# A fused attention and two mixture-of-experts layers: shares laid out by expert, two conversions and a scaling in another order, one earlier load

## The chip, the cores and the metric

The kernel runs on one core of a Trainium2 chip. A core has five engines that work side by side: TensorE (PE in the profile; PEld is its loading of weights), VectorE (DVE), ScalarE (ACT), GpSimd (POOL) and SyncE (SP, which here only issues transfers). Each engine takes its instructions in program order and waits where a semaphore is not there yet. The metric is the device time in microseconds of one execution. Three runs of the kernel before gave 1183.86, 1184.28 and 1185.43 us; their median is 1184.28.

## The reference

Attention over 2 batches of 8 heads with 576 positions and a bias that a small network computes from the positions; on its output (1152 tokens of 512 values) a dense layer with 2048 hidden values and softplus; on that, eight experts with 1024 hidden values each, whose outputs are added with shares P that eight rounds of normalisation make from a gate:

```python
logits = x @ w_gate                      # 1152 x 8
P = np.exp(logits - logits.max())
for _ in range(8):
    P /= P.sum(1, keepdims=True) + 1e-09
    P /= P.sum(0, keepdims=True) + 1e-09
    P *= N / E
for e in range(E):
    out += P[:, e:e + 1] * (np.maximum(x @ w1[e], 0.0) @ w2[e])
```

## The kernel before

*Stages.* The program is written out by hand: each engine's order is the order in which the code issues its instructions, and nothing is rearranged. The first 100 us make the attention's bias: 40 row groups n = 0 to 39 (in `bias_emit`), each summed on TensorE, stored to the DRAM scratch `wt` (five row tiles; wt_72 to wt_76 in the orders below) and read back as `bias` for the first pair of heads at the row groups that the table `READS` names. Other work is hung into these groups by a dictionary `late`: what stands under n is issued after group n's sums and before the reads of that group. Then come eight pairs of heads, nine soft steps s each, which a generator issues (`attention`); its first step, s = 0, is itself issued from `late` at n = 39. `load(i, "kr")` brings the keys of pair i with two transfers of 288 KB on SP's queue into a buffer `raw`; `prep` turns them into a high part `ks` (VectorE, L366) and low parts (POOL, L417).

*Experts.* A unit u is 256 hidden columns: units 0 to 7 are the dense layer, units 8 to 39 the experts, four units each. Every product is computed in three terms from a high part (the operand rounded to fp32r) and a low part (what rounding left): high x high, high x low, low x high. A high part is a copy by ScalarE (`first`, L857), a low part a subtraction by POOL or VectorE (`second`, L861). From unit 12 on, where the experts' shares are ready, units are *gated*: the hidden values are multiplied with the share of their token (VectorE, L880), and units 12 to 38 run the second matrix product in seven half-size products instead of eight (`down_fast`, list `DOWN`), from the hidden blocks B11, B12, B21, B22 and their differences T1 to T4. TensorE runs such a unit in some 22.4 us: the seven products of the up projection (`product`, L818), then the seven of `DOWN` (L994), in the order at = 0 to 6; the product at = 0 needs B11, at = 4 T3, at = 5 B21, at = 6 T4. A unit's start is meant below as the transposition in `turn_last`, behind at = 0.

*Weights.* SP loads a unit's weights into `f` two units ahead. `parts` splits them: ScalarE copies a half to the high part (L730) and, negated, to the low part (L734), and a transfer on POOL's queue then adds the weights to the low part (L735). `weights["high"](u, 1)` is this for the second half of the up weights `wu`, `"highd"` for the down weights `wd`, `"highs"` for the down weights' differences, whose low part lies in `room`. In a unit, POOL issues three of these transfers one behind the other: `wu` of the unit after the next, `wd` and `room`.

*Shares.* `publish` stores the shares from SBUF into the DRAM scratch `pt`, a row of 128 tokens for each pair of token tile t and expert e, row t * 8 + e. `share_of(e, c)` reads half c of expert e's shares back into all 128 partitions (`pb`, 512 tokens); `shares_of` reads both halves. `publish` reads expert 1's two halves and, between them, expert 0's two halves into `raws[2]` and a part of `fs[2]`. `shares_of` is issued at the last unit of an expert, six times, ahead of the next expert. The products of expert 0 (units 8 to 11) went into the accumulators without shares; `weigh_columns` multiplies these accumulators with expert 0's shares in unit 12 (the first scaling, L1038): two on VectorE, two on POOL.

Of the kernel before, what the change touches and what calls it, by code (L numbers as in the profile page):

```python
# [25 lines left out]
E = 8  # L26
# [27 lines left out]
FIRST_STEPS = (39,)  # L54
TABLE_AT = 33
FIRST_LOAD = 3
READS = ((30, 2, ((0, 576),)), (31, 1, ((0, 512),)), (34, 0, ((0, 384),)), (36, 1, ((512, 576),)), (39, 0, ((384, 576),)),
         (39, 3, ((0, 576),)), (39, 4, ((0, 576),)))
G_BUFS = 2
# [54 lines left out]
def attention_moe_moe_kernel(ctx: ExitStack, tc, qT, kT, vN, wpos, w_in, w_out, w_gate, e_w1, e_w2,  # L114
                             psi, logd, rpsi, place, out):
    nc = tc.nc
# [318 lines left out]
    def attention(env, pre, biases, read, ep, bp):  # L435
        pairs, state, load, prep, fixed = pre
# [134 lines left out]
        for s in range(len(seq) + LAG + 2):  # L571
            if s <= AHEAD_STEPS:
                yield
            if s == AHEAD_STEPS:
                sp, xr, beside = env
                for w in range(2):
                    ts = [sp.tile([128, 4, 128], F32R, tag=f"v{x}{w}", name="vx") for x in "hl"]
                    for x in ts:
                        nc.gpsimd.memset(x[:, :, 64:128].bitcast(F32), 0.0)
                    fixed.append(ts)  # L580
            i, r = divmod(s, NT)
            r_now[0] = r
            for w in ORDER[r]:
                if w == "t" and 0 <= s - LAG < len(seq):
                    transp(*seq[s - LAG])
                elif w == "q" and s + 1 < len(seq):
                    qk(*seq[s + 1])
                elif w == "p":
                    for n in range(at[s - 1] if s else 0, at[s]):
                        pv(*parts[n])  # L590
            if LOWFIRST[r]:
                for f in lows:
                    f()
                lows.clear()
            if s < len(seq):
                soft(*seq[s])
            for f in tails + lows:
                f()
            tails.clear()
            lows.clear()  # L600
            if 0 <= s - 1 < len(seq):
                norm(*seq[s - 1], (r - 1) % NT)
            if s == 0:
                load(1, "kr")
            if s == 2:
                prep(0, 5, sp)
            for k, at_r in enumerate(PREPS if i else PREPS1):
                if at_r == r:
                    prep(i + 1, k, sp)
            if r == VLOAD and i + 1 < len(pairs):  # L610
                load(i + 1, "v", sp)
            if i // 2 + 1 < HP and (i % 2, r) in AHEAD:
                read(i // 2 + 1, AHEAD[i % 2, r])
            if s >= AHEAD_STEPS:
                beside(s, ep)


    def experts(m0, accp, xr):
# [6 lines left out]
        U1 = F1 // 256  # L625
# [358 lines left out]
        def down_fast(u):  # L984
# [3 lines left out]
            for at, (n, x, a, b, (c, i)) in enumerate(DOWN):  # L988
# [11 lines left out]
                    nc.vector.tensor_tensor(out=d, in0=banks[x][:, fs_], in1=d, op=ALU.add)  # L1000
                if at == 0:
                    turn_last(u)
                    if u > U1 + UE:
                        weights["high"](u + 1, 1)
                    later.pop()()
                    if (u + 1 - U1) % UE == 0:
                        shares_of((u + 1 - U1) // UE)
                    difference(nc.gpsimd, "T4", "B21", "T2")
                    first("T3")
                    second(nc.gpsimd, "T3")  # L1010
                    second(nc.gpsimd, "B21")
                if at == (2 if u == U1 + UE else 0):
                    if len(tss) < 3:
# [232 lines left out]
        def publish():  # L1246
# [1 line left out]
            tt, sb = bank("t"), raws[2][:, 512:640]  # L1248
            nc.tensor.transpose(tt[0:NT * E, 0:128], pool["prob"].rearrange("p t e -> p (t e)"), ident)
            nc.vector.tensor_copy(sb[0:NT * E], tt[0:NT * E, 0:128])  # L1250
            nc.sync.dma_start(out=pool["pt"], in_=sb[0:NT * E])
            pb["first", 0], pb["first", 1] = raws[2][:, 0:512], fs[2][:, 512:1024]
            for c in range(2):
                share_of(1, c)
                nc.sync.dma_start(out=pb["first", 1 - c].rearrange("p (t n) -> p t n", n=128), in_=shares(0, 4 * (1 - c), 4))

        def shares(e, t, n):
            src = pool["pt"][:]
            return bass.AP(tensor=src.tensor, offset=src.offset + (t * E + e) * 128, ap=[[0, 128], [128 * E, n], [1, 128]])

        def share_of(e, c):
            pb[c] = pool["moe"].tile([128, 512], F32, tag=("s3", "lgt")[c], bufs=1, name="pb")
            nc.sync.dma_start(out=pb[c].rearrange("p (t n) -> p t n", n=128), in_=shares(e, 4 * c, 4))

        def shares_of(e):
            for c in range(2):
# [97 lines left out]
        def unit(u):  # L1364
# [64 lines left out]
            else:  # L1429
                for n, p in enumerate(UP_FAST if fast(u) else UP):  # L1430
                    if u == U1 + UE and n == 5:
                        tss.extend(again(k, [128, 2, 512], F32R) for k in range(2))
                        for i in range(2):
                            weigh_columns(nc.gpsimd, 0, 1 - i)
                    if n == 3 and u == U1 + UE:
                        weigh_columns(nc.vector, 1, 0)
                    if n == 6 and u == U1 + UE:
                        weights["high"](u + 1, 1)
                    if n > 1:
# [115 lines left out]
    with tc.manual_schedule(), ExitStack() as stack:  # L1555
# [37 lines left out]
        one = cst.tile([128, 1], F32, name="one")  # L1593
        late.setdefault(TABLE_AT, []).append(lambda: nc.scalar.activation(one, ident[:, 0:1], AF.Exp))
        late.setdefault(FIRST_LOAD, []).append(lambda: load(1, "qr"))
        for n in FIRST_STEPS:
            late.setdefault(n, []).append(lambda: next(steps))
        with tc.tile_pool(name="btmp", bufs=1) as sp, tc.tile_pool(name="bg", bufs=1) as gp, tc.tile_pool(
# [73 lines left out]
```

## Time and profile before

| what | value |
|---|---|
| median of 3 runs | 1184.28 us (1183.86 to 1185.43) |
| profiled execution | 1183.7 us |
| its span, first to last instruction | 1181.9 us |
| granted clock of TensorE | 1.000 |
| TensorE busy (PE) | 1146.2 us, 97% of the span |
| weight loads (PEld) | 958.6 us, 81% |
| VectorE | 878.2 us, 74% |
| POOL | 840.9 us, 71% |
| ScalarE | 724.6 us, 61% |

The page of the profile describes one execution, whose span is 1.8 us shorter than the execution's own time. TensorE is the fullest engine; it is busy in nearly every slice of the span but the first two. The other engines' idle time costs only where TensorE waits for it. A row of a timeline gives the start in us, the duration, the engine, the line of the code, the operation and its operands; in brackets stands how long the engine was idle before it and what ended that. Rows that follow each other directly are merged, with their count behind an x. TensorE's end times are modelled, and a matmul starts before the one ahead of it has ended, so pairs of rows overlap.

### The profile page before, as it was taken

The page shows a single profiled execution, that of the slowest core. Times are in us where ns is not written, and L with a number is a line of the kernel's source. Part 1 is how long each engine was busy: PE and PEld are TensorE (multiplying, and loading weights), DVE is VectorE, ACT ScalarE, POOL GpSimd, SP SyncE. Part 2 cuts the span into 40 slices and gives each one's busy share as a digit, 9 for nine tenths or more (in the row PEclk, how much of TensorE's full clock was granted, in tenths as well). Part 3 has the DMA queues.
Part 4 walks back from the last instruction along what each step waited for, and adds up shares of the span by engine and source line. Part 5 has one row for each costly group of instructions (what it writes and reads, how often), then busy time and mean ns, then how long its engine had stood idle before and what let it go on. Part 6 is the DMA issues. An engine that isn't in the chain of part 4 may idle for free.

```text
span 1181.9 us, 19793 instructions
## 1 busy us (share of the span) xinstructions
PE 1146.2 (97%) x7289; PEld 958.6 (81%) x7289; DVE 878.2 (74%) x1469; ACT 724.6 (61%) x1190; POOL 840.9 (71%) x858
## 2 busy tenths in 40 slices
PE   5897999999999999999999999999999999999998
PEld 4886999988888887887788887887888887888887
DVE  9986888668888855766777777777777777777773
ACT  8876887865554556335566666665665665666652
POOL 8226777657788874446878878878888887887880
PEclk9999999999999999999999999999999999999999
DMA  5769565022222211126577577567657657658652
GB/s 137 227 172 273 173 199 160 2 71 90 91 90 89 89 54 37 36 36 162 112 154 171 116 152 170 125 136 181 130 123 169 155 114 167 152 121 165 156 110 96
DMA packets 82728, 152.41 MB, mean 129 GB/s; under 512 B 9344, under 2 KB 47304, under 8 KB 82632
## 3 DMA queue, kind: packets, MB, share of 16 engines
q0 software_dynamic: 15984, 58.20, 26.8%
q1 hardware_dynamic: 66072, 92.37, 25.4%
q8 instruction: 57, 0.93, 0.3%
q10 hardware_dynamic: 576, 0.58, 0.2%
q14 instruction: 39, 0.32, 0.1%
HBM read 78.79 MB, written 14.14 MB: 79 GB/s over the span
## 4 chain that ended last, share of the span: by engine, by line
PE 83%; DMA 4%; DVE 4%; issue 3%; POOL 3%; ACT 3%; SPq 0%; DVEq 0%; POOLq 0%; ACTq 0%
PE sum L994 19%; PE t L818 15%; PE sum L1074 10%; PE pv L818 7%; PE op L544 5%; PE pv L1090 4%; PE tail L818 4%; PE pac L269 3%; PE sps L453 3%; PE sum L968 3%; PE tp L503 2%; DMA wu<-f 2%; PE t L836 1%; PE tail L968 1%; DMA room<-f 1%
## 5 line engine op out<-in xcount | busy, mean ns | idle before, releaser
L1000 DVE TENSOR_TENSOR acc<-sum,acc 128x512 f32<-128x512 f32 (+1 forms) x216 | 230.6, 1087 | 91.1 <-PE sum L994 86.7
L818 PE MATMUL t<-room,wu 128*128 128x512 f32 x592 | 160.6, 390 | 0.4 <-DVE u L841 0.4
L1074 PE MATMUL sum<-h,wd 128*128 128x512 f32 x576 | 138.2, 394 | 0.0
L818 PEld LDWEIGHTS t<-room,wu 128*128 128x128 f32 x592 | 111.2, 188 | 23.6 <-DVE u L841 0.9
L1074 PEld LDWEIGHTS sum<-h,wd 128*128 128x128 f32 x576 | 105.5, 188 | 21.9 <-DVE acc L1111 0.4
L818 PE MATMUL pv<-x,wu 128*128 128x512 f32 x444 | 113.1, 390 | 0.0
L730 ACT ACTIVATE wu<-f 128x1024 fp32r<-128x1024 f32 x77 | 81.1, 1054 | 29.6 <-POOL f L725 23.7
L818 PEld LDWEIGHTS pv<-x,wu 128*128 128x128 f32 x444 | 83.1, 188 | 18.0 <-ACT u L846 0.4
L735 POOL DMA_DIRECT2D room<-f x27 | 23.2, 861 | 92.9 <-issue 91.6
L818 PE MATMUL t<-x,wu 128*128 128x512 f32 x296 | 86.4, 392 | 2.2 <-DMA wu<-f 2.2
L861 POOL TENSOR_TENSOR raw<-f,raw 128x512 fp32r<-128x512 f32 x54 | 84.7, 1568 | 0.0
L269 PE MATMUL pac<-bw,m 128*128 128x64 bf16 (+1 forms) x1920 | 66.2, 198 | 18.4 <-DVE bw L241 11.7
L994 PE MATMUL sum<-h,wd 128*128 128x512 f32 x324 | 82.5, 390 | 0.0
L269 PEld LDWEIGHTS <-m 128*128 128x128 bf16 (+1 forms) x1920 | 62.7, 104 | 21.9 <-issue 10.1
L861 POOL TENSOR_TENSOR h<-u,h 128x512 fp32r<-128x512 f32 x55 | 77.8, 1579 | 2.4 <-ACT h L857 2.4
L737 POOL TENSOR_TENSOR wu<-f,wu 128x1024 fp32r<-128x1024 f32 x21 | 53.0, 2526 | 32.6 <-ACT wu L730 31.9
L846 ACT ACTIVATE u<-t 128x512 f32<-128x512 f32 x37 | 22.2, 599 | 85.8 <-PE t L818 85.8
L1111 DVE TENSOR_TENSOR acc<-sum,acc 128x512 f32<-128x512 f32 x80 | 55.1, 689 | 24.7 <-PE sum L1074 24.0
L994 PEld LDWEIGHTS sum<-h,wd 128*128 128x128 f32 x324 | 60.8, 188 | 12.9
L735 POOL DMA_DIRECT2D wu<-f x56 | 49.6, 886 | 26.9 <-ACT h L857 14.7
L994 PE MATMUL sum<-raw 128*128 128x512 f32 x216 | 67.3, 410 | 1.3 <-POOL raw L861 1.3
L818 PEld LDWEIGHTS t<-x,wu 128*128 128x128 f32 x296 | 55.3, 188 | 13.9 <-DMA wu<-f 3.6
(303 smaller groups left out, 3159.3 us busy)
## 6 DMA issues: line engine op xcount, KB each, us to landing
f<-in_e_w_dram SPq DMA_DIRECT2D x128, 256.0 KB, 4.1
wu<-f POOLq DMA_DIRECT2D x56, 512.0 KB, 4.6
wd<-f POOLq DMA_DIRECT2D x28, 512.0 KB, 6.6
room<-f POOLq DMA_DIRECT2D x27, 512.0 KB, 5.3
raw<-in_w_in_dram SPq DMA_DIRECT2D x16, 512.0 KB, 3.6
raw<-in_w_out_dram SPq DMA_DIRECT2D x16, 512.0 KB, 3.6
bias<-wt SPq DMA_DIRECT2D x14, 576.0 KB, 5.9
raw<-in_qT_dram SPq DMA_DIRECT2D x16, 288.0 KB, 5.4
```

The lines of the kernel that those rows point to most:

```text
L269: nc.tensor.matmul(pt[0:n, g], lhs, win(w, (k * (ng + 1) + gw) * NC, [[(ng - gw) * NC, 2], [1, NC]]), start=(k == 0), stop=(k == 2))
L544: nc.tensor.matmul(op[:, 0:n], l, r, start=(part == 0 and k == 0), stop=(part == 8))
L730: nc.scalar.activation(hi, src, AF.Copy)
L735: nc.gpsimd.dma_start(out=lo.bitcast(F32), in_=src, accum_op=ALU.add)
L737: nc.gpsimd.tensor_tensor(out=lo, in0=src, in1=hi.bitcast(F32), op=ALU.subtract)
L818: nc.tensor.matmul(zz, wu(u)[:, a, o:o + 128], xs[xn][b][j], start=(n in (1, 2, 5) and k == 0), stop=(k == 5), skip_group_check=True)
L861: eng.tensor_tensor(out=t[:, 1], in0=full[name], in1=t[:, 0].bitcast(F32), op=ALU.subtract)
L968: nc.tensor.matmul(zr[:, 0:256], xl[:, b, k], wu(u)[:, a, 256 * k:256 * k + 256], start=(n == 0), stop=(n == 3 * KT - 1))
L994: nc.tensor.matmul(banks[x][:, f], ws[wo][:, o + 128 * f:o + 128 * f + 128], h[b][:, ho], start=(n in (1, 5, 2) and k == 0), stop=(k == 2) ...
L1000: nc.vector.tensor_tensor(out=d, in0=banks[x][:, fs_], in1=d, op=ALU.add)
L1074: nc.tensor.matmul(s, lhs, rhs, start=(n == 0), stop=(n == 5))
L1111: nc.vector.tensor_tensor(out=d, in0=o, in1=d, op=ALU.add)
```

## The change

Four pieces. (1) The keys of the second pair are loaded from `late` at row group 35 and no longer at the end of soft step 0. (2) In `down_fast`, the conversion of the second half of the next up weights is issued behind T3's high and low part and no longer behind `turn_last`; this holds for units 13 to 38, 26 of them. (3) `pt` is laid out by expert: row e * 9 + t. `publish` stores it with a transposing address pattern, and each share load reads 512 tokens in one piece of 2,048 bytes per partition, where it read four pieces of 512 bytes. (4) In unit 12 POOL's two scalings are issued at n = 3 of the up products and no longer at n = 5. The order on TensorE and on VectorE stays as it was.

```diff
+NEXT_KEYS = 35
@@ attention
-            if s == 0:
-                load(1, "kr")
@@ down_fast
                 if at == 0:
                     turn_last(u)
-                    if u > U1 + UE:
-                        weights["high"](u + 1, 1)
                     later.pop()()
                     if (u + 1 - U1) % UE == 0:
                         shares_of((u + 1 - U1) // UE)
                     difference(nc.gpsimd, "T4", "B21", "T2")
                     first("T3")
                     second(nc.gpsimd, "T3")
+                    if u > U1 + UE:
+                        weights["high"](u + 1, 1)
                     second(nc.gpsimd, "B21")
@@ publish
-            nc.sync.dma_start(out=pool["pt"], in_=sb[0:NT * E])
+            dst = pool["pt"][:]
+            nc.sync.dma_start(out=bass.AP(tensor=dst.tensor, offset=dst.offset, ap=[[128, NT], [128 * NT, E], [1, 128]]),
+                              in_=sb[0:NT * E])
...
-                nc.sync.dma_start(out=pb["first", 1 - c].rearrange("p (t n) -> p t n", n=128), in_=shares(0, 4 * (1 - c), 4))
+                nc.sync.dma_start(out=pb["first", 1 - c], in_=shares(0, 4 * (1 - c), 4))
@@ shares
-            return bass.AP(tensor=src.tensor, offset=src.offset + (t * E + e) * 128, ap=[[0, 128], [128 * E, n], [1, 128]])
+            return bass.AP(tensor=src.tensor, offset=src.offset + (e * NT + t) * 128, ap=[[0, 128], [1, 128 * n]])
@@ share_of
-            nc.sync.dma_start(out=pb[c].rearrange("p (t n) -> p t n", n=128), in_=shares(e, 4 * c, 4))
+            nc.sync.dma_start(out=pb[c], in_=shares(e, 4 * c, 4))
@@ unit
                     if u == U1 + UE and n == 5:
                         tss.extend(again(k, [128, 2, 512], F32R) for k in range(2))
+                    if n == 3 and u == U1 + UE:
+                        weigh_columns(nc.vector, 1, 0)
                         for i in range(2):
                             weigh_columns(nc.gpsimd, 0, 1 - i)
-                    if n == 3 and u == U1 + UE:
-                        weigh_columns(nc.vector, 1, 0)
@@ the lists of the bias
         late.setdefault(FIRST_LOAD, []).append(lambda: load(1, "qr"))
+        late.setdefault(NEXT_KEYS, []).append(lambda: load(1, "kr"))
```

On SP, at the end of the bias, the queue reads before the change (a row is the line, the operation, what is written from what; `bias<-wt` is a read of a bias, `wt<-extra` a store of one, `raw<-in_kT_dram` the two loads of the keys):

```order
L1578 DMA bias<-wt_72 128x768
L305 DMA wt_72<-extra 512x1x256
L1578 DMA bias<-wt_73 128x128
L305 DMA wt_76<-extra 512x1x128
L305 DMA wt_75<-extra 256x1x128
L305 DMA wt_75<-extra 256x1x256
L1578 DMA bias<-wt_72 128x384
L1578 DMA bias<-wt_75 128x1152
L1580 DMA bias<-wt_76 64x576
L1584 DMA bias<-wt_76 64x512
L1584 DMA bias<-wt_76 64x64
L388 DMA raw<-in_kT_dram 64x1152 x2
```

and after it:

```order
L1579 DMA bias<-wt_72 128x768
L389 DMA raw<-in_kT_dram 64x1152 x2
L306 DMA wt_72<-extra 512x1x256
L1579 DMA bias<-wt_73 128x128
L306 DMA wt_76<-extra 512x1x128
L306 DMA wt_75<-extra 256x1x128
L306 DMA wt_75<-extra 256x1x256
L1579 DMA bias<-wt_72 128x384
L1579 DMA bias<-wt_75 128x1152
L1581 DMA bias<-wt_76 64x576
L1585 DMA bias<-wt_76 64x512
L1585 DMA bias<-wt_76 64x64
```

The keys now stand ahead of ten stores and reads of the bias, right behind the read of 128x768.

On ScalarE, in unit 13 behind `turn_last` (`hl` is its high part, `wu<-f` the two copies of the weights, `h<-u` the high parts of B21 and of T3, `raw<-f` that of T4), before:

```order
L913 ACTIVATE hl<-tail 128x256
L730 ACTIVATE wu_2599<-f_2602 128x1024
L734 ACTIVATE wu_2599<-f_2602 128x1024
L857 ACTIVATE h<-u_7310 128x512
L857 ACTIVATE h<-u_7300 128x512
L857 ACTIVATE raw<-f_4646 128x512
```

and after:

```order
L912 ACTIVATE hl<-tail 128x256
L856 ACTIVATE h<-u_7310 128x512
L856 ACTIVATE h<-u_7300 128x512
L729 ACTIVATE wu_2602<-f_2605 128x1024
L733 ACTIVATE wu_2602<-f_2605 128x1024
L856 ACTIVATE raw<-f_4646 128x512
```

The two copies of the weights have moved behind the high parts of B21 and T3.

On POOL, in the same place (`u<-v,u` is T3's difference and `f<-u,f` T4's; `h<-u,h` are the low parts, T3's first and B21's second; the DMA adds the weights to their low part), before:

```order
L861 TENSOR_TENSOR h<-v_7251,h 128x512
L861 TENSOR_TENSOR raw<-f_4646,raw 128x512
L864 TENSOR_TENSOR u_7300<-v_7251,u_7300 128x512
L735 DMA wu_2599<-f_2602 128x1024
L864 TENSOR_TENSOR f_4646<-u_7310,f_4646 128x512
L861 TENSOR_TENSOR h<-u_7300,h 128x512
L861 TENSOR_TENSOR h<-u_7310,h 128x512
L861 TENSOR_TENSOR raw<-f_4646,raw 128x512
```

and after:

```order
L860 TENSOR_TENSOR h<-v_7251,h 128x512
L860 TENSOR_TENSOR raw<-f_4646,raw 128x512
L863 TENSOR_TENSOR u_7300<-v_7251,u_7300 128x512
L863 TENSOR_TENSOR f_4646<-u_7310,f_4646 128x512
L860 TENSOR_TENSOR h<-u_7300,h 128x512
L734 DMA wu_2602<-f_2605 128x1024
L860 TENSOR_TENSOR h<-u_7310,h 128x512
L860 TENSOR_TENSOR raw<-f_4646,raw 128x512
```

The transfer has moved behind T4's difference and T3's low part, ahead of B21's low part. In unit 12, the two scalings L1038 on POOL stand behind the low part of B22 (`h<-v`) before the change and ahead of it after.

## Rows read from the trace of the kernel before

**Rows 1.** Page, part 1: busy us (share of the span) x instructions, by engine
```profile
PE 1146.2 (97%) x7289; PEld 958.6 (81%) x7289; DVE 878.2 (74%) x1469; ACT 724.6 (61%) x1190; POOL 840.9 (71%) x858
```
**Rows 2.** Waits, PE, 540 to 1182: who <- for whom: us, times, longest
```profile
PE t L818 <- DMA wu<-f: 2.2, 3, 1.0
PE sum L994 <- POOL raw L861: 2.0, 2, 1.3
```
**Rows 3.** Waits of the weight loads (PEld), 574 to 1165, same columns
```profile
PEld sum L994 <- POOL h L861: 6.8, 24, 0.6
...
PEld sum L994 <- DMA room<-f: 3.3, 8, 0.7
```
**Rows 4.** Timeline, SP: start, us, queue, line, op, out<-in, count [idle<-releaser]
```profile
80.93 1.11 SPq L1578 DMA_DIRECT2D bias<-wt  x1
...
94.25 1.23 SPq L388 DMA_DIRECT2D raw<-in_kT_dram  x2
```
**Rows 5.** Timelines of POOL, DVE and PE, 77 to 105 us, same columns
```profile
77.83 1.41 POOL L406 TENSOR_TENSOR ql<-raw,qh 128x576 fp32r<-128x576 f32 x1
...
99.83 0.76 DVE L366 CAST ks<-raw 128x1152 fp32r<-128x1152 f32 x1 [2.22 <-DMA raw<-in_kT_dram]
...
104.51 0.66 PE L503 MATMUL tp<-ident,p 128*128 128x128 f32 x4 [0.84 <-POOL p L480]
```
**Rows 6.** Windows: stretch, us, PE PEld DVE ACT POOL (x), PEclk, DMA share, GB/s
```profile
82.00:86.00 4.00, 3.82 (x96) 3.50 (x91) 1.93 (x3) 1.73 (x3) 0.00 (x0) 1.00 0.42 115
```
**Rows 7.** Timelines of POOL and PE in the first gated unit, u = 12
```profile
549.25 4.77 POOL L1038 TENSOR_TENSOR acc<-acc,raw 128x1024 f32<-128x1024 f32 x2 [2.75 <-DMA raw<-pt]
...
554.55 1.56 POOL L861 TENSOR_TENSOR raw<-f,raw 128x512 fp32r<-128x512 f32 x1
...
556.16 0.73 PE L994 MATMUL sum<-raw 128*128 128x512 f32 x2 [1.28 <-POOL raw L861]
...
565.29 0.74 PE L994 MATMUL sum<-raw,wd 128*128 128x512 f32 x2 [0.69 <-POOL raw L861]
```
**Rows 8.** Windows; page, part 6: out<-in, queue, count, KB each, us to landing
```profile
535.50:537.50 2.00, 2.00 (x11) 1.65 (x10) 0.98 (x2) 2.00 (x3) 0.99 (x2) 1.00 0.34 81
690.00:691.50 1.50, 1.50 (x8) 1.06 (x7) 1.50 (x4) 1.50 (x2) 1.50 (x2) 1.00 0.93 319
...
pb<-pt SPq DMA_DIRECT2D x14, 256.0 KB, 6.8
...
v<-in_psi_dram ACTq DMA_DIRECT2D x1, 288.0 KB, 3.5
```
**Rows 9.** PE's timeline at 725; landing of L735's transfers issued 714.77 and 647.44
```profile
725.59 0.62 PE L818 MATMUL pv<-x,wu 128*128 128x512 f32 x2
...
DMA to landing us min/median/max: 9.7/9.7/9.7
...
DMA to landing us min/median/max: 4.6/4.6/4.6
```
**Rows 10.** Timelines of ACT, DVE, POOL (unit from 644.20), PE (from 711.53)
```profile
645.84 1.05 ACT L734 ACTIVATE wu<-f 128x1024 fp32r<-128x1024 f32 x1
646.79 1.14 ACT L857 ACTIVATE h<-u 128x512 fp32r<-128x512 f32 x2
...
645.93 0.68 DVE L880 SCALAR_TENSOR_TENSOR u<-t,pb 128x512 f32<-128x512 f32 x1
...
647.44 0.88 POOL L735 DMA_DIRECT2D wu<-f  x1 [0.61 <-ACT h L857]
...
649.31 2.83 POOL L861 TENSOR_TENSOR h<-u,h 128x512 fp32r<-128x512 f32 x2
...
718.28 0.73 PE L994 MATMUL sum<-h,raw 128*128 128x512 f32 x2
```
**Rows 11.** Landing of L735's transfers into room, issued 661.28 and 683.7
```profile
DMA to landing us min/median/max: 6.1/6.1/6.1
...
DMA to landing us min/median/max: 5.3/5.3/5.3
```

## Prediction

> **What bounds the kernel now.** I read four views, in this order. The page's first part: TensorE is busy for 97% of the span [rows 1], so only a place where TensorE itself waits can give time back. Then the waits of its matmuls and of its weight loads in the experts' stage [rows 2, 3]: the matmuls stand still in few places, 2.2 us in three waits for a weights' transfer and 2.0 us in two waits for a low part from POOL; the weight loads wait more often, 24 times for a low part from POOL and 8 times for the transfer into `room`. Then the timeline at the start of attention, where TensorE is far from full, for what is late there [rows 4, 5]. Last the timelines of the first gated unit, of an experts' boundary and of a plain unit [rows 7, 9, 10]. One more measure is needed: a wait that the timeline prints costs more than it prints. Two matmuls of 512 columns in a row take 0.62 us [rows 9]; one start follows another after 0.23, so a row's end is 0.39 after its start; the idle time counts from that end, 0.16 late. And the second matmul behind a wait starts 0.11 late again: such a pair takes 0.73 us and not 0.62 [rows 7]. So **each printed wait costs 0.27 us on top**.
>
> **The change, part by part.**
>
> *The keys of the second pair.* Their two loads are now issued behind the bias read that ends on SP's queue at 80.93 + 1.11 = 82.04, not at 94.25 [rows 4]. Their buffer is free by then (POOL's last read of it began at 77.83 and takes 1.4 [rows 5]). VectorE's conversion of these keys waits 2.22 us for the landing and starts at 99.83 [rows 5]. Behind it stand, on VectorE, the softmax of the next tile and, on POOL, the keys' low parts and then the probabilities whose transposition TensorE awaits at 104.51 [rows 5]. Landed 5.5 us after the issue, as now (94.25 to just before 99.83), the keys are there at 87.6, ten microseconds early; that chain then starts when VectorE is free, 2.22 us sooner. Next late is the read of the last bias, which lands just before the keys do now, about a microsecond before the earlier softmax wants it. What is moved past: ten bias stores and reads on SP's queue. From 82 to 86 us the DMA engines are busy for 0.42 and move 115 GB/s [rows 6]; in the other 0.58 x 4 us they could move some 635 KB at that rate per busy time, and the two loads are 590 KB. So the stores behind them are hardly held up. Bounds: from 0 (the stores lose what the keys gain) to 2.3; I take **2.1 us**, near the upper end, because the room is there. From 105 us on TensorE has work without gaps, so it stays.
>
> *Shares by expert.* A share load brings 256 KB into 128 partitions, until now as four pieces of 512 bytes per partition, from now on as one of 2,048. Where two to four of them run alone, the chip moves 81 GB/s at a DMA share of 0.34; weights in pieces of 1 and 2 KB run at 319 GB/s and 0.93 [rows 8]. So the engines wait for pieces, not for bytes. That the same bytes go to all partitions is not the brake: the load of psi, 288 KB, also one row for all partitions but in long pieces, lands in 3.5 us, a share in 6.8 [rows 8]. With a quarter of the pieces a share should move in about 0.8 to 1.8 us and not in 3.4 (256 KB at 319 or at some 150 GB/s, against 81). The page "DMA: Bandwidth & Descriptors" of the Trainium skill (Specifications) says that from 512 bytes on a piece runs at line rate; by it the new layout would move nothing faster. The row of 81 GB/s speaks against it; what the time would be by it stands under the rivals, from rows.
>
> Who waits for that. *(a)* At six boundaries of experts two share loads are issued just ahead of POOL's weights' transfer for the next unit. That transfer then lands after 9.7 us and not 4.6 [rows 9], and three times TensorE waits for it, 2.2 us printed [rows 2]. With shares that are done when it is issued, it lands in time: 2.2 + 3 x 0.27 = **3.0 us**. *(b)* In the first gated unit POOL waits for the fourth share before it scales two accumulators, from 549.25, 4.77 us [rows 7]. Behind these two on POOL stand a weights' transfer and the low part of T2, from 554.55, for which TensorE waits 1.28 us at 556.16; and some ten operations on the low part of T4, for which it waits 0.69 at 565.29 [rows 7].
>
> *First scaling earlier on POOL.* It now stands one low part (1.3 us) ahead. By the bounds above the fourth share lands at 541 to 544 and not at 549, so the two scalings are over by 549, the low part that they have passed by 550 (TensorE uses it after 558), and the low part of T2 starts when ScalarE's high part is there, about 551.4, three microseconds sooner. It needs 1.3 sooner. The chain to T4 is then some 2.5 us sooner and needs 1.5 + 0.7. Both waits go: 2.0 + 2 x 0.27 = **2.5 us**.
>
> *Conversions in 26 units.* On ScalarE the two copies of the next weights' second half (1.05 us each) now stand behind the high parts of B21 and T3; on POOL that weights' transfer stands behind T4's difference and T3's low part. Worked out on the plain unit at 644 us [rows 10]: VectorE ends B21's product at 646.61, so its high part ends at 647.2, T3's at 647.8, the two copies at 649.7 (now 646.89). POOL needs no wait for T3's low part, which starts at 647.9 and not at 649.31: **1.4 us sooner**. TensorE waits for just that part in 24 of 26 units, 0.28 us on the weight load [rows 3]; on the matmuls the pair behind it takes 0.73 instead of 0.62 and starts 0.03 late [rows 10], 0.14 us. Twenty such and one of 0.44 are 3.2 us. On the other side POOL's transfer starts 0.55 behind the copies, as now (646.89 to 647.44), at 650.25, 2.8 us later. It lands 4.6 later at 654.8; TensorE wants it at about 655.8: covered by 1 us, and a wait beyond. What POOL has behind it comes 0.3 us later (650.86 for 650.56), down to three transfers one behind the other, the last of them into `room`. So that one lands 0.3 later, while TensorE arrives 0.14 sooner. Usually it lands 5.3 us after its issue, 0.8 before the late ones [rows 11], about 0.7 ahead of TensorE; 0.26 is left. But in 8 units TensorE waits for it already [rows 3], and there 0.44 more is added: 8 x 0.44 = 3.5, with a little for the others 3.6. So this part is 3.2 won and 3.6 lost, **0.4 us lost**; between 2.5 won (POOL makes good the 0.3) and 2 lost.
>
> **The sum**: -2.1 - 3.0 - 2.5 + 0.4 = -7.2 us. On the profiled execution's 1183.7 us that is 1176.5; the median of the runs, 1184.28, is 0.6 above it: **1177.1 us**, with 1174.8 to 1179.5 for this case alone.
>
> **Rivals.**
>
> *1. The shares stay slow* (their rate goes by bytes of the repeated row, as the page's rule would also have it). For it: the 81 GB/s are measured on just such loads. Against it: psi's load. Then the three boundaries keep their waits (the weights' transfer is issued later but was held up by the shares anyway), and in the first gated unit the low part that the scalings have passed comes behind the wait until 549.25 too, ahead of T2: 1.25 us more of waiting. -2.1 + 1.25 + 0.4: 1183.8 us.
>
> *2. The burst into `room` comes too late in every unit* (the other side). The place is POOL's transfer behind the copies; it decides where the burst comes over 0.3 + 0.26 = 0.56 us later than now. At 0.8 later, 18 units wait 0.24 + 0.11 and 8 wait 0.5 more: 6.3 + 4.0 = 10.3 us on top of the sum, 1187.4 us. For it: 8 of 26 units are at the edge now [rows 3]. Against it: the 0.3 follows from operations whose lengths are all in the rows.
>
> *3. T3's wait goes and nothing takes its place*, because POOL's pauses (0.61 us ahead of the transfer now [rows 10]) absorb the 0.3. Then the 3.6 are not lost: 1173.5 us.
>
> **How the numbers follow.** Forecast 0.66, rival 1 0.11, rival 2 0.08, rival 3 0.15. The range from 1173.0 to 1181.5 holds the forecast with keys that give nothing, and rival 3: about 0.8. A measurement of this kernel tells 0.2%, 2.4 us, from no change: faster are the forecast and rival 3, 0.81; within 0.2% rival 1 and a mild rival 2, 0.13; slower the rest of rival 2, 0.06.
>
> **What the profile of after would show.** Keys: VectorE's conversion without a wait for the keys' landing, near 97.6, and TensorE's transposition at 102.3. Shares: landing in 3 to 4 us, none of the waits of t<-x,wu for a weights' transfer. First gated unit: the scalings before 549 and no wait for a low part from POOL. Conversions: the weight loads' waits for T3's low part gone, and those for `room` more and longer, some 0.6 us each. Wrong it would be if shares still land after 6 us, if the units between boundaries grow beyond 22.4 us, or if VectorE waits for a bias near 92 or 98 us.

## The result, and the profile after

The changed kernel takes **1175.07 us** (median of 4 runs, 1174.61 to 1175.23) against 1184.64 us of the kernel before on the same chip: a ratio of 0.9919, 95% interval 0.9901 to 0.9936. That is 9.6 us less; 7.2 were forecast, and the time lies in the range. Two of the forecast's four terms were right, two were wrong, in opposite directions.

The first part of the page after, with the columns of [rows 1]:

```profile
PE 1142.6 (97%) x7289; PEld 962.3 (82%) x7289; DVE 878.7 (75%) x1469; ACT 724.6 (62%) x1190; POOL 841.6 (72%) x858
```

The other engines do the same work as before; the span, 1172.8 us, lost 9.1 us of TensorE's waiting and of its longer runs behind waits. Where, is read from the transposition in `turn_last`, the start of a unit as counted above. The timeline of PE has it for units 12, 13 and 38, before:

```profile
552.08 0.27 PE L979 MATMUL tail<-ident,gl 128*128 128x128 f32 x1
...
576.86 0.27 PE L979 MATMUL tail<-ident,gl 128*128 128x128 f32 x1
...
1141.45 0.27 PE L979 MATMUL tail<-ident,gl 128*128 128x128 f32 x1
```

and after:

```profile
551.82 0.27 PE L978 MATMUL tail<-ident,gl 128*128 128x128 f32 x1
...
574.53 0.27 PE L978 MATMUL tail<-ident,gl 128*128 128x128 f32 x1
...
1132.50 0.27 PE L978 MATMUL tail<-ident,gl 128*128 128x128 f32 x1
```

| stretch | before, us | after, us | gained | forecast |
|---|---|---|---|---|
| up to unit 12 (the keys) | 552.08 | 551.82 | 0.3 | 2.1 |
| unit 12, the first gated one | 24.79 | 22.72 | 2.1 | 2.5 |
| units 13 to 37 | 564.59 | 557.97 | 6.6 | 3.0 - 0.4 = 2.6 |
| unit 38 to the end of the span | 40.47 | 40.32 | 0.1 | 0 |

The first row is counted from the start of the trace, which is not the same moment in both: the first softmax step stands at 86.28 us before and at 85.73 after. Counted from that step, the dense layer's first unit starts 172.71 us later before and 172.84 after, so the keys show no gain here.

Matmuls and weight loads wait for less. The waits of PE from 540 us on and of PEld from 570 to 1165 us, after:

```profile
PE sum L993 <- DMA room<-f: 0.6, 3, 0.3
PE pv L967 <- DVE u L879: 0.3, 1, 0.3
PE sum L993 <- POOL raw L860: 0.2, 1, 0.2
...
PEld sum L993 <- DMA room<-f: 3.4, 8, 0.7
```

Of [rows 2], the three waits for a weights' transfer are gone, and of the two for a low part one is left, of 0.2 us. Of [rows 3], the 24 waits for T3's low part are gone, and `room` is waited for 8 times as before, 3.4 us in place of 3.3.

The places of [rows 9, 10], after: the matmuls that used T3's low part run without a gap (0.62 us and not 0.73), and the weights' transfer issued at the boundary of unit 19, at 714.27, lands in 4.6 us:

```profile
715.17 0.62 PE L993 MATMUL sum<-h,raw 128*128 128x512 f32 x2
...
DMA to landing us min/median/max: 4.6/4.6/4.6
```

At the keys something new stands. The timelines of SP and of DVE before:

```profile
84.99 0.55 SPq L305 DMA_DIRECT2D wt<-extra  x1
...
89.52 0.76 DVE L466 CUSTOM_DVE_ANT_0 p<-sps,bias 128x576 f32<-128x576 f32 x1 [0.41 <-DMA bias<-wt]
```

and after:

```profile
80.54 0.84 SPq L1579 DMA_DIRECT2D bias<-wt  x1
81.50 1.16 SPq L389 DMA_DIRECT2D raw<-in_kT_dram  x2
85.88 0.57 SPq L306 DMA_DIRECT2D wt<-extra  x1
86.91 0.32 SPq L1579 DMA_DIRECT2D bias<-wt  x1
...
90.93 0.76 DVE L467 CUSTOM_DVE_ANT_0 p<-sps,bias 128x576 f32<-128x576 f32 x1 [2.36 <-DMA bias<-wt]
...
98.94 0.76 DVE L367 CAST ks<-raw 128x1152 fp32r<-128x1152 f32 x1
```

The conversion of the keys no longer waits; but the third softmax step now waits 2.36 us for a bias, where it waited 0.41 at 89.52. The store at 85.88 waits for the bias read of 80.54 to have landed (it writes into the scratch that this reads), as the waits of SP's queue from 78 to 100 us say. It is issued 5.34 us after that read; before, 4.06 us (80.93 to 84.99):

```profile
SPq L306 <- DMA bias<-wt: 6.8, 2, 3.7
```

The next bias read stands behind that store.

### The profile page after: what moved, and what is told of

Same layout as the page of the kernel before. It is cut to its first block, busy times and chain, and to the rows that moved or that the text cites. A ratio compares the mean times of both kernels' runs of the same rounds, so it can differ in the third digit from the quotient of the medians.

```text
span 1172.8 us, 19768 instructions
## 1 busy us (share of the span) xinstructions
PE 1142.6 (97%) x7289; PEld 962.3 (82%) x7289; DVE 878.7 (75%) x1469; ACT 724.6 (62%) x1190; POOL 841.6 (72%) x858
## 4 chain that ended last, share of the span: by engine, by line
PE 83%; DVE 5%; DMA 5%; issue 2%; ACT 2%; POOL 2%; SPq 0%; DVEq 0%; ACTq 0%; POOLq 0%
PE sum L993 21%; PE t L817 15%; PE sum L1073 10%; PE pv L817 7%; PE op L545 5%; PE pv L1089 4%; PE tail L817 4%; PE sps L454 3%; PE sum L967 3%; PE tp L504 3%; DMA room<-f 2%; PE t L835 1%; DMA bias<-wt 1%; PE tail L967 1%; PE pac L270 1%
## 5 line engine op out<-in xcount | busy, mean ns | idle before, releaser
L860 POOL TENSOR_TENSOR h<-u,h 128x512 fp32r<-128x512 f32 x55 | 80.9, 1476 | 2.4 <-ACT h L856 2.4
L471 ACT ACTIVATE p<-p,sm 128x576 f32<-128x576 f32 x72 | 55.7, 773 | 15.9 <-DVE sm L467 12.9
```

What stands on the lines that cost most here:

```text
L471: nc.scalar.activation(p, p, AF.Exp, bias=sm[:, o:o + 1], scale=-1.0, accum_out=sm[:, 2 + o:3 + o])
L860: eng.tensor_tensor(out=t[:, 1], in0=full[name], in1=t[:, 0].bitcast(F32), op=ALU.subtract)
```

## The experiments

Times are medians, ratios are against the kernel before on the same chip. "Unit 12" and "units 13 to 37" are read from each trace as in the table above. The start of a trace shifts from run to run (the first softmax step stands at 85.4 to 87.7 us), so the early stage is measured from the first softmax step on.

### Each part alone on the kernel before

**b_keys**, the first piece of the diff alone:

> The kernel before with the earlier keys alone. Theory of the prediction: the conversion of the keys no longer waits 2.22 us and nothing takes its place, so TensorE's first transposition in the dense layer comes 2.1 us sooner and the time is 1182.5 us against 1184.6. Rival, drawn from the trace of the changed kernel: the keys slow the bias read that is in flight ahead of them, the store behind waits for that read, and the softmax step that uses the next bias waits some 2.4 us near 91 us where it waited 0.4; the first unit then starts within 0.5 us of before and the time is 1184.2 to 1184.9.

Measured: 1183.87 us, ratio 1.0000 (0.9991 to 1.0010). The rival came true: the keys' conversion starts without a wait at 99.03, the third softmax step waits:

```profile
90.56 0.76 DVE L467 CUSTOM_DVE_ANT_0 p<-sps,bias 128x576 f32<-128x576 f32 x1 [1.49 <-DMA bias<-wt]
```

The first unit starts 172.52 us after the first softmax step, against 172.71 before. The earlier keys are worth 0.2 us here, nothing that can be measured.

**b_shares**, the third piece alone (layout by expert, stores and loads):

> The kernel before with the layout by expert alone. Theory of the prediction: a share lands in 3 to 4.5 us, the three waits at the boundaries go (3.0 us), and in the first gated unit the fourth share lands by 545.5, so that the scalings are over some 3.7 us sooner and both waits for low parts go or nearly go (2 to 2.5 us): 1179 to 1180 us. Rival: at the boundaries the waits went in the changed kernel because the weights' transfer is issued later there and not because the shares are faster; then this kernel keeps waits at units 19, 23 and 31 and gains 2.5 us at most: 1182 us.

Measured: 1178.97 us, ratio 0.9955 (0.9940 to 0.9970); 5.4 us of the 9.6. Unit 12 takes 22.32 us, units 13 to 37 561.68, 2.9 less; units 19, 23 and 31 take 22.43 to 22.45 where they took 23.70, 23.17 and 23.46. In the waits of PE from 540 us on neither the weights' transfer nor a low part is left:

```profile
PE sum L994 <- DMA room<-f: 0.5, 1, 0.5
PE pv L968 <- DVE u L880: 0.3, 1, 0.3
```

So the shares alone account for both places, the boundaries and the first gated unit.

**b_high**, the second piece alone (`weights["high"](u + 1, 1)` behind `second(nc.gpsimd, "T3")`):

> The kernel before with the later conversions alone. Theory of the prediction: T3's low part is no longer waited for, but the transfer into room lands 0.3 us later and TensorE waits 0.44 us more for it in eight units: 0.4 us slower, 1185.0 us. Rival, from the trace of the changed kernel: room's issue hangs on ScalarE's copy and not on POOL's earlier transfers, so it moves with TensorE, plain units take 22.23 us and not 22.42, and the time is 3 to 4 us shorter, 1181 us; the three waits at the boundaries of 0.5 to 1 us stay, since the slow shares hold the weights' transfer up whenever it is issued.

Measured: 1181.63 us, ratio 0.9979 (0.9965 to 0.9992). The rival came true: plain units take 22.26 us at the median, before 22.43. The boundary units gain nothing (22.99 on average, as before): TensorE comes sooner and waits longer for the same late transfer, five times, 2.4 us printed, where there were three of 2.2.

**b_scale**, the fourth piece alone:

> The kernel before with POOL's two scalings ahead of B22's low part alone, shares as slow as before. Theory of the prediction (its first rival's working): the fourth share still lands at 549.2, the low part that stood ahead of the scalings now comes behind them, and everything behind is 1.25 us later: TensorE's wait at the first gated unit grows from 1.28 to some 2.5 us, 1185.9 us. Rival: POOL has room behind the scalings and the time stays within 0.4 us of 1184.6.

Measured: 1185.09 us, ratio 1.0011 (1.0001 to 1.0020). The theory came true: the scalings start at 549.81, and T2's low part, behind them and B22's, is late:

```profile
557.94 0.73 PE L994 MATMUL sum<-raw 128*128 128x512 f32 x2 [2.92 <-POOL raw L861]
```

Unit 12 takes 26.41 us, 1.6 more than before (1.25 were forecast), in a profile of an execution of 1187.1 us, 2 us above the median. With slow shares the earlier place costs.

### One part undone in the changed kernel

**a_noscale**, the fourth piece undone:

```diff
-                    if n == 3 and u == U1 + UE:
-                        weigh_columns(nc.vector, 1, 0)
                         for i in range(2):
                             weigh_columns(nc.gpsimd, 0, 1 - i)
+                    if n == 3 and u == U1 + UE:
+                        weigh_columns(nc.vector, 1, 0)
```

> The changed kernel with POOL's two scalings back behind B22's low part (n = 5). Theory of the prediction: the earlier scalings spare the low part of T2 and the chain to T4 some 1.3 us, so without them the first gated unit is longer, by some 0.5 to 1 us: 1175.6 to 1176 us. Rival, from the run with the layout by expert alone, whose first gated unit took 22.32 us against 22.72 in the changed kernel: the earlier scalings make POOL wait 4.26 us for the share with B22's low part behind them, and cost 0.4 us: 1174.7 us, with no wait for a low part in that unit.

Measured: ratio 0.9905 (0.9882 to 0.9927), 1175.53 us; the runs can't tell it from the changed kernel's 0.9919. The traces can: unit 12 takes 22.26 us here and 22.32 in b_shares, both with the scalings behind B22's low part, and 22.72, 22.75 and 22.63 in the three with fast shares that have them ahead. POOL's timeline, first of the changed kernel, then of this one:

```profile
545.61 4.78 POOL L1037 TENSOR_TENSOR acc<-acc,raw 128x1024 f32<-128x1024 f32 x2 [4.26 <-DMA raw<-pt]
550.35 1.29 POOL L860 TENSOR_TENSOR h<-v,h 128x512 fp32r<-128x512 f32 x1
...
552.20 1.57 POOL L860 TENSOR_TENSOR raw<-f,raw 128x512 fp32r<-128x512 f32 x1
```

```profile
544.03 1.28 POOL L860 TENSOR_TENSOR h<-v,h 128x512 fp32r<-128x512 f32 x1 [3.61 <-ACT h L856]
545.36 4.78 POOL L1037 TENSOR_TENSOR acc<-acc,raw 128x1024 f32<-128x1024 f32 x2
...
550.68 1.58 POOL L860 TENSOR_TENSOR raw<-f,raw 128x512 fp32r<-128x512 f32 x1
```

Unit 12 starts at 551.82 in the first trace and at 550.89 in the second, so 0.93 us are to be taken off the first one's times before they are compared. In the changed kernel the fourth share lands at 545.6. B22's low part could start at 545.0 there (544.03 + 0.93), and half of it would fall into the wait for the share; the earlier scalings push it behind them. T2's low part (the last row of each) then starts 0.39 us after the unit's start and not 0.21 before it, 0.6 us later, and so does what follows on POOL. At the end of that chain TensorE waits for T4's low part, in PE's timeline of the changed kernel:

```profile
562.96 0.73 PE L993 MATMUL sum<-raw,wd 128*128 128x512 f32 x2 [0.16 <-POOL raw L860]
```

With 0.27 us on top, as the prediction reckons a printed wait, these are 0.43 of the 0.45 us.

**a_noshares**, the third piece undone:

> The changed kernel with the layout by token tile as before, shares in four pieces of 512 bytes. Theory: the boundaries' gain and the first gated unit's hang on the share loads alone; the six boundary units take some 23.0 us each and not 22.32 (+4 us), the first gated unit 26.4 and not 22.7 (+3.7 us), 1182.8 us. Rival: with the weights' transfer issued later the slow shares are done in time at the boundaries; then only the first gated unit is longer: 1178.8 us.

Measured: ratio 0.9995 (0.9977 to 1.0013). Without the new layout the other three parts together are worth nothing. The ten runs reach from 1179.84 to 1188.59 us; in the profiled one, of 1187.86, the boundary units take 23.26 us on average (22.32 with it), unit 12 28.69, more than either theory said; the section on the hardware comes back to it.

**a_nokeys**, the first piece undone:

> The changed kernel with the keys of the second pair loaded where they were. Theory of the prediction: the conversion waits 2.2 us for them again and the time is 2.1 us longer, 1177.2 us. Rival, from the run with the earlier keys alone (no measurable gain, a wait of some 2 us for a bias in place of the one for the keys): within 0.5 us of the changed kernel, 1174.7 to 1175.6 us, and the softmax step near 90 us waits 0.4 us for its bias and not 2.4.

Measured: ratio 0.9913 (0.9890 to 0.9935); the changed kernel has 0.9919. The conversion waits 2.16 us for the keys again, the softmax step at 91.13 only 0.60 us for its bias, and the time is the same. (The absolute median, 1175.92, belongs to a series in which the kernel before took 1186.74.)

**a_pool**, a measured delay ahead of the burst into `room`:

```diff
                     second(nc.gpsimd, "B21")
+                    if u > U1 + UE:
+                        t = h["B21"]
+                        nc.gpsimd.tensor_tensor(out=t[:, 1, 0:256], in0=full["B21"][:, 0:256],
+                                                in1=t[:, 0, 0:256].bitcast(F32), op=ALU.subtract)
```

> The changed kernel with half of B21's low part computed a second time on POOL in units 13 to 38, some 0.65 us of POOL's time ahead of its three transfers on end (the result is the same). Theory of the prediction: whatever comes ahead of the burst delays the landing in room by as much, and from a delay of about 0.5 us on every unit waits: the units grow by 0.15 to 0.65 us each, in all by some 8 us: 1183 us. Rival: the landing in room hangs on ScalarE's copy and on the queue and not on POOL's chain ahead, so that plain units stay within 0.05 us of 22.24: 1175.5 us.

Measured: ratio 0.9960 (0.9946 to 0.9974); units 13 to 37 take 564.81 us, 6.8 more than in the changed kernel. The burst's first transfer is issued 12.95 us after a unit's start (12.10 in the changed kernel), `room` lands at 23.3 (22.4; medians of 25 units), and the weight loads wait in nearly every unit, waits of PEld from 574 to 1165 us:

```profile
PEld sum L993 <- DMA room<-f: 14.6, 23, 1.1
```

So the prediction's mechanism holds: a delay of the burst's start by 0.85 us moves the landing in `room` by about as much, and it costs. From which delay on it costs, this one size does not tell. The rival falls.

### Three more, on causes

**b_halfkeys**, one of the two key loads early, the other at its old place:

```diff
+NEXT_KEYS = 35
...
             if s == 0:
-                load(1, "kr")
+                load(1, "kr", halves=(1,))
...
+        late.setdefault(NEXT_KEYS, []).append(lambda: load(1, "kr", halves=(0,)))
```

> The kernel before with one of the two key loads early, the other where it was. Theory: the keys' bytes slow the bias read in flight ahead of them, so half the bytes cost half: the third softmax step starts 4.1 us after the first (3.3 with both late, 4.9 with both early, averages of five profiles each), and the conversion still waits for the second half, some 1.5 to 2 us. Rival: it is the place in SP's order and not the bytes: the third step comes as late as with both, 4.9 us.

Measured: ratio 1.0000 (0.9988 to 1.0012). The third softmax step starts 3.97 us after the first, between the 3.3 and the 4.9, as the theory has it. That alone decides little: single profiles with late keys reach from 2.96 to 4.08, and here the step waits last for TensorE's transposition and not for its bias. A nearer measure is the time from the bias read in flight to the store that waits for it. It is 4.05 to 4.39 us in the eight profiles without keys right behind that read, 4.79 to 5.48 in the five with both loads there, and 4.66 here: about half the delay for half the bytes, in one profile. The conversion waits 0.38 us for the second half, less than expected.

**b_1k**, shares in two pieces of 1,024 bytes: row (t // 2 * 8 + e) of 256 tokens.

```diff
...
-            return bass.AP(tensor=src.tensor, offset=src.offset + (t * E + e) * 128, ap=[[0, 128], [128 * E, n], [1, 128]])
+            return bass.AP(tensor=src.tensor, offset=src.offset + (t // 2 * E + e) * 256, ap=[[0, 128], [256 * E, n // 2], [1, 256]])
...
```

> The kernel before with shares laid out in pairs of token tiles, two pieces of 1,024 bytes per partition in place of four of 512 (publish stores them with five transfers). Theory: a share load's time goes by its pieces, about 160 a microsecond; it landed after 6.8 us with 512 pieces, 4.4 with 128, so with 256 it lands after 5.2 us; at the boundaries the waits for the weights' transfer are nearly gone (units of 22.45 to 22.6 us and not 22.99). Rival: from 1,024 bytes on the bytes count: 4.4 us as with 2,048; or pieces do not matter and the order of the rows does: 6.8 us.

Measured: ratio 0.9983 (0.9974 to 0.9992); the share loads land after 6.6 us at the median (6.8 with 512-byte pieces, 4.4 with 2,048). The theory falls, and the first half of the rival with it (4.4 us from 1,024 bytes on). Windows (columns as in [rows 6]) in which share loads run nearly alone at the same boundary, of the kernel before, of this one and of the changed kernel:

```profile
715.00:718.50 3.50, 3.50 (x17) 2.70 (x16) 2.17 (x3) 1.75 (x4) 3.50 (x4) 1.00 0.25 72
```

```profile
715.50:719.00 3.50, 3.50 (x17) 2.71 (x16) 2.17 (x2) 1.75 (x4) 3.50 (x4) 1.00 0.66 68
```

```profile
711.90:713.40 1.50, 1.50 (x9) 1.23 (x8) 1.24 (x2) 1.50 (x3) 1.50 (x2) 1.00 0.58 195
```

Half as many pieces, and the same 68 to 72 GB/s; one run of 2,048 bytes, and 195. So the number of pieces is not what counts. The DMA engines' busy share does not tell the rate either: 72 GB/s stand at a share of 0.25, 68 at 0.66. In both slow layouts the pieces of one load lie apart (4,096 and 8,192 bytes), in the fast one they are one run. Whether the length of a run counts or the distance between the pieces, no run here tells.

**best_mid and best_burst**, meant to beat both kernels. best_mid is a_noscale with the keys issued between the reads of the last two biases:

```diff
-NEXT_KEYS = 35
+NEXT_KEYS = -1
...
                 if n == at:
+                    for fn in late.get(-1, ()) if t == 4 else ():
+                        fn()
                     read(0, t, spans)
```

> The changed kernel with the scalings at n = 5 again, and the keys issued between the reads of the last two biases (row tiles 3 and 4), some 2 us ahead of where they were before the change. Theory: the bias reads up to row tile 3 are undisturbed, so the third softmax step waits 0.4 us as before the change; the keys land near 98 and their conversion waits 0.5 us and not 2.2; the last bias lands 1.2 us later and takes part of it back. The first unit starts 0.5 to 1 us sooner after the first softmax step than with the keys at either other place (172.8 us on average of the profiles so far); in all 0.987 to 0.991 of the time before. Rival: the stage is bound by the bytes that the keys and biases bring together, and any place gives the same: 172.8 again.

Measured: 1173.40 us, ratio 0.9912 (0.9899 to 0.9925), not to be told from the changed kernel. Unit 12 takes 22.27 us, 0.45 less, as in a_noscale; the third softmax step waits only 0.23 us, the keys' conversion 1.24, and the first unit starts 172.69 us after the first softmax step: no gain from this place either.

best_burst is best_mid with the burst's first part ahead of the four differences:

```diff
-        DOWN_JOBS = {1: (("mixd", 1, 0),), 3: (("high", 2, 0),), 4: (("highd", 1, 0),)}
+        DOWN_JOBS = {1: (("high", 2, 0), ("mixd", 1, 0)), 4: (("highd", 1, 0),)}
```

> The kernel of the run before, with the conversion of the first half of the weights after the next (and its transfer, the first of the burst into room) issued ahead of the four operations on the down weights' differences, in place of behind them. Theory, from the run with 0.65 us more on POOL (16 waits for room, plain units longer by 0.24): the landing in room hangs on the start of the burst; with its first transfer some 3 us earlier room lands by 21.7 us after a unit's start, no unit waits for it, the plain units' mean falls from 22.32 to 22.24 and the time by 1.5 to 2 us more. Rival: room's own issue, behind ScalarE's copy at 16.9, sets the landing then, and its 3.1 us alone on the queue would give 20 to 20.5; or the weights of the unit after the next have not landed yet when ScalarE reaches the copies, ScalarE then holds up T4's neighbours and the units grow.

Measured: 1180.12 us, ratio 0.9970 (0.9961 to 0.9980), 6.7 us slower than best_mid. The first transfer does start 3 us earlier (8.9 us after a unit's start) and the second lands at 17.6 in place of 19.3. The third, into `room`, is issued where it was, at 17.1 (16.9 in best_mid), so the rival was right on what sets its issue. But it then takes 6.1 us where it took 5.4, and not the 3.1 that the rival gave it alone; it lands at 23.3 and not at 22.4 (medians of 25 units). That neither theory foresaw. POOL's and SP's timelines in unit 16, which starts at 641.87:

```profile
654.89 0.87 POOL L736 DMA_DIRECT2D wd<-f  x1
658.97 0.86 POOL L736 DMA_DIRECT2D room<-f  x1 [3.20 <-issue]
...
659.69 3.37 SPq L685 DMA_DIRECT2D f<-in_e_w_dram  x4
```

and SP's in unit 17 of the changed kernel, which starts at 663.98:

```profile
683.40 2.72 SPq L683 DMA_DIRECT2D f<-in_e_w_dram  x4
```

SP's loads of the next weights wait for the second transfer of the burst, which lands 4.7 us after 654.89, and follow its landing by 0.1 us in both kernels. They come 17.8 us after the unit's start here and 19.4 there, so they run beside `room` for some 5.4 us and not for 2.9. That is the likely reason why `room` takes longer; no run moves these loads alone, so it is not shown.

## Why the prediction was right, and where it was not

**The boundaries (3.0 us): right**, in mechanism and size. b_shares alone takes 1.25, 0.74 and 1.01 us off units 19, 23 and 31: 3.0, from 2.2 printed. The rule that a printed wait costs 0.27 us more holds here.

**The first gated unit (2.5 us): right in its cause, 2.1 measured.** The fast shares give 2.47 (24.79 to 22.32 in b_shares) without the moved scalings; these give 0.45 back. The step that failed is "the fourth share lands at 541 to 544". It landed at 545.6: the loads ran beside the weights' transfers there and not alone (the DMA share is 0.95 to 1.26 from 536 to 546 us), and the order of POOL's two steps that was right for 544 is wrong for 545.6, because B22's low part can start at 545.0. The first rival's picture of that order with slow shares held: b_scale lost 1.6 us where 1.25 was worked out.

**The keys (2.1 us): wrong, 0.3 at most and within the spread.** The mechanism was half seen: the wait for the keys did go. The step that failed is "So the stores behind them are hardly held up". It was worked out from the mean DMA share of four microseconds [rows 6], 0.42, as free room for 590 KB. What counted was not the room but one read in flight: the keys come right behind it on SP's queue, it lands later, and a store that waits for its landing goes out later, with the next bias behind it on SP's queue. The time from that read to the store is 4.05 to 4.39 us in the eight profiles without the keys there and 4.79 to 5.48 in the five with them. That it is the bytes and not the place, b_halfkeys supports with one profile (4.66). The prediction had named the sign by which to know it, VectorE waiting for a bias near 92 us. The softmax is about 1.5 us later there (3.3 to 4.9 us between its first and third step), the keys are ready 0.5 us sooner than before (13.1 us after the first step for 13.6, averages of five profiles each), and the first unit, 172.8 us after it for 173.1, is within the spread of either group (172.0 to 173.6 and 172.7 to 173.5).

**The conversions (0.4 us lost): wrong, 3.6 won.** Here the third rival came true, "T3's wait goes and nothing takes its place", though not for its reason. Two sizes failed. The gain of a plain unit was put at 0.14 us; it is 0.19 (22.43 to 22.24 at the median); why, no run tells. In all 25 units that would be 4.7 us, an estimate, for 3.2. And the loss at `room`, put at 3.6, is about 1.1 (6.6 in units 13 to 37, less the boundaries' 3.0, are 3.6; these are 1.1 short of 4.7): the step "What POOL has behind it comes 0.3 us later" was off. In unit 17 of the changed kernel, ACT and POOL:

```profile
668.44 1.04 ACT L733 ACTIVATE wu<-f 128x1024 fp32r<-128x1024 f32 x1
...
667.80 1.30 POOL L860 TENSOR_TENSOR h<-u,h 128x512 fp32r<-128x512 f32 x1
669.77 0.88 POOL L734 DMA_DIRECT2D wu<-f  x1 [0.68 <-ACT wu L733]
670.38 1.61 POOL L860 TENSOR_TENSOR h<-u,h 128x512 fp32r<-128x512 f32 x1
```

The transfer is issued 0.29 us behind the second copy (668.44 + 1.04 to 669.77), where the prediction carried over the 0.55 of the trace before. B21's low part starts 6.40 us after the unit's start (663.98), 6.37 before. The burst's first transfer follows at 12.10 for 12.03, and `room` lands at 22.41 for 22.48 (medians of 25 units). So the 0.3 was 0.03 to 0.07. That the mechanism was right all the same, a_pool shows: 0.85 us at the same place cost 6.8 us, where rival 2 had put 0.8 us at 10.3. No run takes the conversions alone out of the changed kernel; the 3.6 rests on b_high, 2.6 us less in units 13 to 37 than before, and on the changed kernel against b_shares, 3.7 less there.

**The sum** came near by luck, because the errors have opposite signs (keys and first unit by the table): 1.8 too much on the keys and 0.4 on the first gated unit, 4.0 too little on the conversions. Part of the gain hangs on two parts together: with slow shares the boundary units get nothing from the conversions, with fast ones 0.1 to 0.2 us each. That a_noshares is no faster than the kernel before comes mostly from the scalings: in its profile unit 12, with slow shares and the earlier scalings, takes 3.9 us more than before.

**The page's rule.** That from 512 bytes on a piece runs at line rate (the Trainium skill, "DMA: Bandwidth & Descriptors", Specifications) does not hold for these loads: 72 GB/s in pieces of 512 bytes, 68 in pieces of 1,024, 195 in one run of 2,048. The prediction was right to go by the row against it, but its own reading, that the engines wait for pieces, does not hold either.

## What to carry to other kernels

An early load is not free because the transfer engines have idle shares: look at what is in flight just ahead of it and at what may not start before that has landed. When a step is moved past a wait, compare the time at which its own input comes with the time at which the passed step's input comes; a difference of a microsecond decides it, and it must be taken from loads that run beside what will run then. Before a small delay is carried down a chain, find the next place in it where the engine waits for something else: there the delay ends, or, in a burst of transfers that follow without a pause, it does not.

## What the hardware showed beside this

**TensorE's clock.** In a_noshares TensorE stood still for 3.4 us in unit 12. Behind that the granted clock was 0.50, 1.2 GHz, for some 6 us. Its timeline and the windows:

```profile
559.30 1.22 PE L993 MATMUL sum<-raw 128*128 128x512 f32 x2 [3.37 <-POOL raw L860]
560.33 2.76 PE L1089 MATMUL pv<-wd,hl 128*128 128x512 f32 x6
...
556.00:559.00 3.00, 0.00 (x0) 0.00 (x0) 0.67 (x1) 0.20 (x1) 3.00 (x4) 0.91 0.23 44
559.00:562.00 3.00, 2.70 (x6) 2.16 (x7) 1.23 (x1) 0.89 (x2) 3.00 (x4) 0.50 0.70 131
```

Six matmuls took 2.76 us in place of 1.54, and unit 12 was 2.3 us longer than in b_scale, where the matmuls behind the wait ran at the full clock (1.53 us for such six) and TensorE's printed waits in the unit were no shorter (3.6 us for 3.4). The same fall stands in the changed kernel's early stage, behind the wait for the bias, windows:

```profile
90.00:92.00 2.00, 0.24 (x1) 0.25 (x2) 1.03 (x5) 0.27 (x1) 0.06 (x1) 0.89 1.00 206
92.00:94.00 2.00, 2.00 (x10) 1.79 (x10) 1.68 (x6) 1.84 (x5) 1.44 (x2) 0.50 0.57 164
```

It is in most profiles of that stage, with the keys early or late, though not in the one before and not in b_high; how much of the spread of the first unit's start is its doing, no run here separates.
